# Gram and score products on four quarters of the array, and a mixture layer's activations squared once

## The chip, the cores and the metric

The kernel runs on one core of one Trainium2 chip, as one launch. The metric is the device time of that launch in microseconds (us). Three runs of the kernel before took 984.56, 985.13 and 986.95 us; the median is 985.13 us.

## The reference

Three layers follow one another, on 4 batches of 768 tokens, 8 heads of 48 dimensions (so 384 features):

```python
# delta-rule attention, per head, token by token
k_n = k / (norm(k) + 1e-6)
for t in range(768):
    y[t]  = q[t] @ state
    state = state + beta[t] * outer(k_n[t], v[t] - state.T @ k_n[t])
# first mixture layer, 3072 tokens, 384 -> 2048 -> 384
r = maximum(x @ w_in, 0);  x = (r * r) @ w_out
# second mixture layer: 8 experts, 384 -> 1024 -> 384, one per token
keep = x @ w_skip > 0;  e = argmax(x @ w_gate);  g = max softmax(x @ w_gate)
out = x;  out[keep] += g * (maximum(x @ w1[e], 0) @ w2[e])
```

All data is float32, except that the weights of the first mixture layer come as float64.

## The kernel before

**Attention.** The recurrence is worked in chunks of 64 tokens. A chunk needs, for each head, the 64 by 64 matrix of the keys' products with one another (called G, the Gram matrix) and that of the keys with the queries (P, the scores), both over the 48 dimensions. A *unit* `i` is two chunks, and a *step* `(i, c)` with c from 0 to 3 is one chunk for half of the 32 heads of all batches: 16 heads, held as 8 pairs. There are 6 units, so 24 steps. In a pair one head's 48 dimensions lie on partitions 0 to 47 and the other's on 64 to 111.

`Attn.gram` (lines 241 to 279) makes G and P of one step. `load` (line 249) brings keys and queries of 8 pairs into the tile `gkq`, 128 columns a pair: 64 of keys, then 64 of queries. `spread` (line 253, twice: rows 0 to 47 and rows 64 to 111) copies the keys into the tile `kb`, whose other entries are zero, so that each pair's keys stand block-diagonally as 112 rows by 128 columns. `mm` (line 262), called for each half of the pairs, multiplies: one product of 112 rows gives both heads' G and P as 128 by 128 outputs, four pairs in one PSUM bank. The profile counts two matmul records for a float32 product, so the 8 products of a step are 16 records in two pieces of 8. `copy` (lines 266 and 267) brings G and P into SBUF on ACT, and `store` (line 277) writes the diagonal blocks of G to DRAM.

`sysinv` (lines 297 to 358) takes the blocks of all four steps of a unit back from DRAM (`prep`, line 307), one system to a partition, and inverts them in 31 dependent pairs of DVE instructions (lines 335 and 336). `merge` (products at lines 384 and 398) joins blocks of 32 to blocks of 64. `kv` loads keys and values, and `loadq` (line 426) fetches the queries once more into `qp`, out of the same array as `gkq`: rows of 64 floats with gaps of 64 between them. `recur` holds the four groups of small products of a step, W, U, Y and DS (lines 477, 491, 501, 519). Each of these groups is 16 products and 32 records.

**First mixture layer.** Six units of 512 tokens by 16 slices of the hidden dimension give 96 hidden chunks `f`. `Moe1.w` loads a slice of weights (line 668) and splits it into a rounded part `whi` (ACT, line 672) and a remainder `wlo` (DVE, line 675). `Moe1.h` (lines 698 to 726) makes 9 products into the one PSUM bank `p_h` (line 708), the relu on ACT into the single buffer `r` (713), the rounded square `gh` on ACT (717), the full square `g`, a single buffer, on DVE (721), and the remainder `gl = g - gh` on DVE (724). `Moe1.y` makes 12 products out of `gh`, `gl`, `whi` and `wlo` (738). Weights from float64 are rebuilt as float32 by `Conv.chunk` (lines 548 to 612), 16 chunks on ACT, DVE and POOL, before the first hidden chunk.

**Second mixture layer.** `Moe2` splits the experts' weights and runs sorted blocks of 128 tokens (lines 1051 to 1081).

**What sets the order.** The instructions of attention and first mixture layer are put into one written order per engine by a list scheduler that runs while the kernel is built (`Order`, lines 72 to 166). Each piece has an engine, an estimated duration, an urgency and the pieces it follows; the scheduler steps a model of the engines forward and emits the piece that can start first, the more urgent one among those close together. On the chip each engine's instructions then run in exactly that order. Pieces that write PSUM take banks in rotation: seven (`BANKS`) up to the first hidden chunk, then the three of tag "a". Until then the scheduler also inserts products without use (line 1262) which keep TensorE busy. `schedule` adds attention steps and hidden chunks with urgencies at a fixed spacing `L`, and units 1 to 5 of attention run among the chunks of the mixture layer.

Of the kernel before, what the change touches and what calls it, by code (L numbers as in the profile page):

```python
# [8 lines left out]
F32 = mybir.dt.float32  # L9
# [19 lines left out]
C = 64  # L29
# [42 lines left out]
class Order:  # L72
# [16 lines left out]


    def add(s, urgency, piece, after=(), behind=(), at=0.0):
        k = len(s.p)
        after, behind = tuple(after), tuple(behind)
        s.p.append((urgency, piece, after, behind, at))
        s.n.append(0)
        s.succ.append([])
        for j in (*after, *behind):
            if j not in s.issued:
                s.n[k] += 1
                s.succ[j].append(k)  # L100
        if not s.n[k]:
            s.enable(k)
        return k
# [14 lines left out]
    def run(s, until=None, slack=0.35):  # L118
        todo = set(range(len(s.p)) if until is None else until) - set(s.issued)
        while todo:  # L120
            best = {}
            for k, t in s.ready.items():
                u, (e, d, f, *x), *_ = s.p[k]
                t = max(t, s.free[e])
                if e == PE and x:
                    tag = s.tags[s.turn % len(s.tags)]
                    l = s.taken[tag]
                    if len(l) >= s.count[tag]:
                        j = l[-s.count[tag]] + 1
                        if j not in s.issued:  # L130
                            continue
                        t = max(t, s.end[j])
                best.setdefault(e, []).append((t, u, k))
# [8 lines left out]
            if e == PE:  # L142
                if s.clock:
                    c, n = s.clock, x[1] if len(x) > 1 else 0
                    if t > 54.83 or 3.5 < t < 19.48:
                        b = max(s.free[e], 54.83 if t > 54.83 else 3.5)
                        while c.end(b, 0.11) <= t + 0 or b >= t and c.low(b, d, n):
                            b = c.run(b, 0.11, 256)
                            s.dummy()
                        t = max(t, b)  # L150
                    d = c.run(t, d, n) - t
                if x:
                    s.taken[s.tags[s.turn % len(s.tags)]].append(k + x[0] - 1)
                    s.turn += 1
# [14 lines left out]
class Attn:  # L169


    def __init__(s, ctx, tc, kq, kv, bs, xT, psum):
        s.tc = tc
        s.nc = nc = tc.nc
        s.kq, s.kv_, s.bs, s.xT, s.psum = kq, kv, bs, xT, psum

# [10 lines left out]
        W = 8 * D + 16  # L187
        s.gq, s.gb = ([c1.tile([128, 8, 128], F32, name=f"{n}{i}") for i in range(2)] for n in ("gkq", "kb"))

# [51 lines left out]
    def gram(s, i, ci):  # L241
# [4 lines left out]
        def load():  # L246
            st["q"], st["b"] = s.q0[ci] if i == 0 and ci < 2 else s.gq[ci % 2], s.gb[ci % 2]
            for a in range(2):
                nc.sync.dma_start(out=st["q"][a * 64:a * 64 + D].rearrange("p a b -> p (a b)"), in_=s.kq[c, a, :, h8 * 128:(h8 + 8) * 128])

        def spread(r):
            f = nc.vector.tensor_copy if r and not i else nc.scalar.copy
            f(out=st["b"][r:r + D, :, 64 - r:128 - r], in_=st["q"][r:r + D, :, 0:64])

        def mm(b):
            if b == 0:
                s.P[i, ci] = s.pP.tile([128, 8, 64], F32, name="P")
                s.G[i, ci] = s.pG.tile([128, 8, 64], F32, name="G")
            st[b] = gp = s.psum([128, 4, 128])
            for q in range(4):  # L260
                p = b * 4 + q
# [146 lines left out]
    def kv(s, i, ci):  # L408
# [206 lines left out]
class Moe1:  # L615
# [82 lines left out]
    def h(s, f):  # L698
# [28 lines left out]

# [421 lines left out]

def build(tc, kq, kv, bs, w, wsg, w1, w2, out):  # L1150
    nc = tc.nc
    with ExitStack() as ctx:
# [14 lines left out]
        with ExitStack() as cm:  # L1167
# [19 lines left out]
            cv, tail = cm.enter_context(ExitStack()), cm.enter_context(ExitStack())  # L1187
            A = Attn(ca, tc, kq, kv, bs, xT, psum)
            ew = ctx.enter_context(ExitStack())
# [15 lines left out]
def schedule(A, open_V, open_M, clear, E, free, ca, tail, ew, manual):  # L1205
# [11 lines left out]
    def gram(i, c, ul, u):  # L1217
        m, l = 4 * i + c, A.gram(i, c)
        old = at(gr, m - 2, 5)
        x = [o.add(ul, l[0], old if i else [], at(gr, m - 1, 0))]  # L1220
        x += o.chain(u, l[1:3], x + old)
        x += o.chain(u, l[3:], x[-1:], at(gr, m - 1, 5) + at(mg, m - NG, 2) + at(kv, m - NP, 6))
        gr[m] = x
# [104 lines left out]
    def m_unit(i):  # L1328
        for f in range(NF):
# [72 lines left out]
def layout(q, k, v, beta):  # L1402
# [5 lines left out]

    kq = np.stack([dm(k), dm(q)], axis=4).reshape(12, 2, D, 16 * 128)
    kv = np.stack([tm(k), tm(v)], axis=2)  # L1410
    bs = beta.reshape(2, 2, 4, 2, 6, 2, 2, 32)[:, :, :, ::-1].transpose(4, 6, 5, 0, 3, 1, 2, 7).reshape(6, 128, 32)
    return dict(kq=np.ascontiguousarray(kq), kv=np.ascontiguousarray(kv), bs=np.ascontiguousarray(bs))

# [20 lines left out]
```

## Time and profile before

| | |
|---|---|
| median of three runs | 985.13 us |
| the profiled execution | 984.34 us, span 982.6 us |
| TensorE (PE) busy | 91% |
| VectorE (DVE) busy | 71% |
| ScalarE (ACT) busy | 57% |
| GpSimd (POOL) busy | 34% |
| mean granted TensorE clock | 0.957 |

The span runs from the first to the last instruction; 1.74 us of the profiled execution lie outside it. A busy share is an average over stretches with different limits. Four stretches can be told apart here: attention's first unit and the rebuilding of the weights (0 to 168 us), the mixture layer with the other units of attention (168 to about 645 us), the mixture layer nearly alone (645 to 766 us), and the experts (766 us to the end). PE is matmul, PEld the load of its stationary operand, SP the queue that issues most DMAs.

### The profile page before, as it was taken

What the parts mean: (1) busy time and instruction counts of PE and PEld (TensorE: products, weight loads), DVE (VectorE), ACT (ScalarE), POOL (GpSimd) and SP (SyncE); (2) the same over time, 40 slices, a digit from 0 to 9 for tenths busy, and PEclk for the clock granted to TensorE, in tenths of its full rate; (3) what the DMA queues carried; (4) which work ended last, traced back from release to release, by engine and by line L of the source; (5) the groups of instructions that cost most, each with busy time, mean ns of one, the idle gap of its engine ahead of it and who ended that gap; (6) DMA issues with size and microseconds to landing.
All of it is one profiled execution on the core that took longest, in us unless ns stands there. A gap on an engine that the chain in (4) does not pass through costs nothing. (4 is left out here: it accounts for less than half of the span.)

```text
span 982.6 us, 23182 instructions
## 1 busy us (share of the span) xinstructions
PE 895.4 (91%) x8594; PEld 784.6 (80%) x8594; DVE 695.2 (71%) x1311; ACT 564.3 (57%) x1039; POOL 335.0 (34%) x445
## 2 busy tenths in 40 slices
PE   8577876999989998999989997999999999999996
PEld 6575765887778887888878876888899889898996
DVE  7898677889966998489955998553786523845563
ACT  6824845766577556775576545665665323745562
POOL 9805462134424332433326331531250230111011
PEclk9787996998999999999999999999999999999999
DMA  8937766653586457533765346433591232844661
GB/s 246 271 81 211 226 193 180 159 140 97 141 207 161 113 124 212 153 103 107 195 152 148 94 124 170 108 104 90 171 313 50 72 122 98 292 131 143 226 218 46
DMA packets 148698, 152.12 MB, mean 155 GB/s; under 512 B 92344, under 2 KB 127129, under 8 KB 148560
## 3 DMA queue, kind: packets, MB, share of 16 engines
q1 hardware_dynamic: 132336, 92.84, 33.9%
q0 software_dynamic: 16224, 57.56, 19.9%
q8 instruction: 72, 1.18, 0.5%
q14 instruction: 66, 0.54, 0.2%
HBM read 116.63 MB, written 35.91 MB: 155 GB/s over the span
## 5 line engine op out<-in xcount | busy, mean ns | idle before, releaser
L668 POOL DMA_DIRECT2D wraw<-wc x96 | 53.6, 559 | 293.0 <-DVE wlo L675 203.1
L713 ACT ACTIVATE r<-p_h 128x512 f32<-128x512 f32 x96 | 57.5, 599 | 111.7 <-PE p_h L708 45.6
L672 ACT CAST whi<-wraw 128x778 fp32r<-128x778 f32 x96 | 81.3, 847 | 68.1 <-PE p_y L738 65.2
L675 DVE TENSOR_TENSOR wlo<-wraw,whi 128x778 fp32r<-128x778 f32 x96 | 96.2, 1003 | 24.6 <-ACT whi L672 24.0
L721 DVE TENSOR_TENSOR g<-r 128x512 f32<-128x512 f32 x96 | 66.6, 694 | 56.6 <-ACT r L713 56.4
L738 PE MATMUL p_y<-whi,gl 128*128 128x394 f32 x384 | 88.3, 352 | 6.6 <-DVE gl L724 6.4
L708 PE MATMUL p_h<-xh,wlo 128*128 128x512 f32 x288 | 83.7, 399 | 9.3 <-DVE wlo L675 9.2
L708 PE MATMUL p_h<-xh,whi 128*128 128x512 f32 x288 | 89.2, 418 | 2.5 <-ACT r L713 2.3
L738 PE MATMUL p_y<-whi,gh 128*128 128x394 f32 x384 | 89.5, 355 | 0.0
L738 PE MATMUL p_y<-wlo,gh 128*128 128x394 f32 x384 | 87.2, 350 | 0.0
L336 DVE TENSOR_TENSOR Xsys<-Xsys,Osys 128x31 f32<-128x31 f32 (+15 forms) x186 | 81.8, 440 | 6.4
L335 DVE TENSOR_TENSOR Osys<-Asys,Xsys 128x31 f32<-128x31 f32 (+15 forms) x186 | 80.3, 432 | 3.9
L708 PE MATMUL p_h<-xl,whi 128*128 128x512 f32 x288 | 82.6, 395 | 0.0
L724 DVE TENSOR_TENSOR gl<-g,gh 128x512 fp32r<-128x512 f32 x96 | 71.5, 745 | 15.1 <-ACT gh L717 4.4
L738 PEld LDWEIGHTS p_y<-whi,gl 128*128 128x128 f32 x384 | 71.9, 195 | 9.5 <-DVE gl L724 9.3
L1081 POOL DMA_INDIRECT out<-eo,ex x21 | 23.4, 1116 | 161.8 <-DVEq L979 93.9
L738 PEld LDWEIGHTS p_y<-whi,gh 128*128 128x128 f32 x384 | 69.1, 191 | 6.7
L708 PEld LDWEIGHTS p_h<-xh,wlo 128*128 128x128 f32 x288 | 53.3, 189 | 26.0 <-DVE wlo L675 14.8
L451 POOL TENSOR_TENSOR qp<-P,mask 64x512 f32<-64x512 f32 x48 | 67.9, 1415 | 13.4 <-PE p_a L501 9.5
L738 PEld LDWEIGHTS p_y<-wlo,gh 128*128 128x128 f32 x384 | 72.2, 194 | 0.0
L708 PEld LDWEIGHTS p_h<-xl,whi 128*128 128x128 f32 x288 | 54.5, 189 | 13.0 <-DVE xl L694 0.2
L445 POOL TENSOR_TENSOR x<-x,nw 64x384 f32<-64x384 f32 x48 | 47.0, 980 | 47.3 <-DVE nw L292 44.3
(247 smaller groups left out, 2017.2 us busy)
## 6 DMA issues: line engine op xcount, KB each, us to landing
wraw<-wc POOLq DMA_DIRECT2D x96, 389.0 KB, 3.9
raw<-in_w SPq DMA_DIRECT2D x16, 768.0 KB, 5.2
r<-in_w SPq DMA_DIRECT2D x24, 512.0 KB, 4.8
r<-in_w SPq DMA_DIRECT2D x32, 384.0 KB, 6.1
gkq<-in_kq SPq DMA_DIRECT2D x48, 192.0 KB, 4.1
wc<-cvo SPq DMA_DIRECT2D x16, 389.0 KB, 7.2
ex<-xs SPq DMA_DIRECT2D x24, 193.0 KB, 3.2
k<-in_kv POOLq DMA_DIRECT2D x48, 96.0 KB, 3.8
```

The lines of the kernel that those rows point to most:

```text
L335: v.tensor_tensor(out=tmp, in0=A[:, k, k + 1:32].unsqueeze(2).to_broadcast(sh), in1=X[:, k, None, 0:k + 1].to_broadcast(sh), op=ALU.mult)
L336: v.tensor_tensor(out=X[:, k + 1:32, 0:k + 1], in0=X[:, k + 1:32, 0:k + 1], in1=tmp, op=ALU.subtract)
L445: nc.gpsimd.tensor_tensor(out=x, in0=x, in1=st["n"][r].unsqueeze(2).to_broadcast([64, 8, D]), op=ALU.mult)
L451: nc.gpsimd.tensor_tensor(out=QP[r, 1 - t], in0=P[r], in1=s.mask[r, None, :].to_broadcast([64, 8, 64]), op=ALU.mult)
L668: nc.gpsimd.dma_start(out=st["t"], in_=s.wc[f])
L672: nc.scalar.copy(out=s.W[f][0], in_=st["t"])
L675: nc.vector.tensor_tensor(out=s.W[f][1], in0=st["t"], in1=s.W[f][0].bitcast(F32), op=ALU.subtract)
L708: nc.tensor.matmul(ps, lhsT=w[:, k * 128:k * 128 + 128], rhs=x[k], start=(n == 0), stop=(n == 8))
L713: nc.scalar.activation(out=r, in_=st["p"], func=AF.Relu)
L721: nc.vector.tensor_tensor(out=g, in0=st["r"], in1=st["r"], op=ALU.mult)
L724: nc.vector.tensor_tensor(out=s.g[f][1], in0=st["g"], in1=s.g[f][0].bitcast(F32), op=ALU.subtract)
L738: nc.tensor.matmul(s.ys[t], lhsT=g[:, t * 128:t * 128 + 128], rhs=w[:, DM:], start=first, stop=last)
```

## The change

The Gram products use quarters of the array: each of the 16 heads of a step has its own product, 48 rows by 64 columns of keys against 128 columns of keys and queries. Even pairs go to one PSUM bank and odd pairs to a second; the host exchanges the two heads of every odd pair in the array `kq`, so that the four products of two pairs stand on four different quarters (rows 64 or 0, columns 0 or 64). One piece `mm` takes both banks at once (the new `Order.banks`). The tile `kb`, both `spread` copies and the memsets for them go. The queries for `qp` come from an input of their own, `qf`, without gaps. In the mixture layer ACT makes the full square `g`, and then a second ACT instruction rounds it into `gh`; DVE only makes the remainder.

```diff
@@ class Order
+    def banks(s, n=1):
+        t, used = 0.0, {}
+        for r in range(n):
+            tag = s.tags[(s.turn + r) % len(s.tags)]
+            l, k = s.taken[tag], used.get(tag, 0) - s.count[tag]
+            used[tag] = used.get(tag, 0) + 1
+            if len(l) + k >= 0:
+                if k >= 0 or l[k] + 1 not in s.issued:
+                    return None
+                t = max(t, s.end[l[k] + 1])
+        return t
@@ Attn.init
-        for t in s.q0:
-            nc.vector.memset(t[32:64], 0.0)
-        for t in s.gb:
-            nc.gpsimd.memset(t, 0.0)
-        for i, t in enumerate(s.gq):
-            (nc.vector, nc.gpsimd)[i % 2].memset(t[32:64], 0.0)
@@ Attn.gram
-        def spread(r):
-            f = nc.vector.tensor_copy if r and not i else nc.scalar.copy
-            f(out=st["b"][r:r + D, :, 64 - r:128 - r], in_=st["q"][r:r + D, :, 0:64])
-        def mm(b):
...
-                nc.tensor.matmul(gp[:, q, :], lhsT=st["b"][0:112, p, :], rhs=st["q"][0:112, p, :], start=True, stop=True)
+        def mm():
...
+            st[0], st[1] = s.psum([128, 4, 128]), s.psum([128, 4, 128])
             for q in range(4):
+                for b in range(2):
+                    for a in range(2):
+                        f = (1 - a ^ b) * 64
+                        nc.tensor.matmul(st[b][a * 64:a * 64 + 64, q, :], lhsT=st["q"][f:f + D, 2 * q + b, 0:64], rhs=st["q"][f:f + D, 2 * q + b, :], start=True, stop=True, tile_position=(f, a * 64))
-            nc.scalar.copy(out=G[:, b * 4:b * 4 + 4], in_=gp[:, :, 0:64])
-            nc.scalar.copy(out=P[:, b * 4:b * 4 + 4], in_=gp[:, :, 64:128])
+            nc.scalar.copy(out=G[:, b::2], in_=gp[:, :, 0:64])
+            nc.scalar.copy(out=P[:, b::2], in_=gp[:, :, 64:128])
-        return [(SP, 1.0, load, 1.1), (ACT, 0.45, lambda: spread(0)), (ACT if i else DVE, 0.55, lambda: spread(64)), (PE, 0.87, lambda: mm(0), 1, 1792), (ACT, 0.55, lambda: copy(0)), (PE, 0.87, lambda: mm(1), 1, 1792), (ACT, 0.55, lambda: copy(1)), (SP, 1.9, store, 0.8)]
+        return [(SP, 1.0, load, 1.1), (PE, 0.9, mm, 1, 1536, 2), (ACT, 0.75, lambda: copy(0)), (ACT, 0.75, lambda: copy(1)), (SP, 1.9, store, 0.8)]
@@ Attn.kv
-                nc.sync.dma_start(out=QP[a * 64:a * 64 + D, a], in_=s.kq[c, a, :, h8 * 128:(h8 + 8) * 128].rearrange("p (a w) -> p a w", w=128)[:, :, 64:128])
+                nc.sync.dma_start(out=QP[a * 64:a * 64 + D, a].rearrange("p a w -> p (a w)"), in_=s.qf[c, a, :, h8 * 64:(h8 + 8) * 64])
@@ Moe1.h
-            nc.scalar.activation(out=s.g[f][0], in_=st["r"], func=AF.Square)
+            nc.scalar.copy(out=s.g[f][0], in_=st["g"])
-            nc.vector.tensor_tensor(out=g, in0=st["r"], in1=st["r"], op=ALU.mult)
+            nc.scalar.activation(out=g, in_=st["r"], func=AF.Square)
-        return [(PE, 1.95, mm), (ACT, 0.5, relu), (ACT, 0.55, hi), (DVE, 0.62, sq), (DVE, 0.62, lo)]
+        return [(PE, 1.95, mm), (ACT, 0.5, relu), (ACT, 0.55, sq), (ACT, 0.55, hi), (DVE, 0.62, lo)]
@@ schedule: gram
+        q = o.add(u, l[1], x[:1], at(gr, m - 1, 5) + at(mg, m - NG, 2) + at(kv, m - NP, 6))
+        c0 = o.add(u, l[2], [q])
+        c1 = o.add(u, l[3], [q, c0])
@@ schedule: hidden chunks
-            h.append(o.add(u, l[1], h[:1] + (hs[n - 1][2:4] if n else [])))
-            h.append(o.add(u, l[2], h[1:2] + ([ys[n - 2]] if n > 1 else [])))
-            h.append(o.add(u, l[3], h[1:2] + ([hs[n - 1][4]] if n else [])))
-            h.append(o.add(u, l[4], h[2:4]))
+            h.append(o.add(u, l[1], h[:1] + (hs[n - 1][2:3] if n else [])))
+            h.append(o.add(u, l[2], h[1:2] + (hs[n - 1][3:5] if n else [])))
+            h.append(o.add(u, l[3], h[2:3] + ([ys[n - 2]] if n > 1 else [])))
+            h.append(o.add(u, l[4], h[3:4]))
```

## Rows read from the trace of the kernel before

**Rows 1.** Busy us by stretch: PE, PEld, DVE, ACT, POOL, clock, DMA share, GB/s.
```profile
168.00:645.00 477.00, 447.06 (x5250) 385.69 (x5250) 376.24 (x762) 299.86 (x577) 178.52 (x230) 0.98 0.55 143
645.00:766.00 121.00, 120.65 (x824) 107.79 (x823) 77.33 (x135) 72.10 (x117) 29.70 (x37) 1.00 0.44 139
```
**Rows 2.** Waits, 168 to 645 us: who for whom, us in total, times, longest.
```profile
PE p_h L708 <- DVE wlo L675: 9.2, 11, 1.9
PE p_y L738 <- DVE gl L724: 6.4, 7, 2.2
ACT r L713 <- DVE g L721: 30.8, 11, 4.6
```
**Rows 3.** Timeline of PE, 322 to 325 us: start, us, what; a hidden chunk.
```profile
322.18 0.86 PE L708 MATMUL p_h<-xh,whi 128*128 128x512 f32 x3
...
324.25 0.88 PE L738 MATMUL p_y<-whi,gh 128*128 128x394 f32 x4
```
**Rows 4.** Timeline of PE, 409 to 413 us: the two pieces of a step.
```profile
409.49 1.05 PE L262 MATMUL p_a<-gkq,kb 112*128 112x128 f32 x8
410.47 1.10 PE L477 MATMUL p_a<-lt,k 128*48 128x64 f32 x32
411.50 1.16 PE L262 MATMUL p_a<-gkq,kb 112*128 112x128 f32 x8
412.42 0.94 PE L708 MATMUL p_h<-xh,whi 128*128 128x512 f32 x3
```
**Rows 5.** Timeline of PE, 315 to 318 us: groups on parts of the array.
```profile
315.42 0.69 PE L384 MATMUL p_a<-Tn,G 32*32 32x32 f32 x32
316.04 1.15 PE L501 MATMUL p_a<-qp,x 128*64 128x64 f32 x32
317.13 0.77 PE L398 MATMUL p_a<-lt,Z 32*32 32x32 f32 x32
```
**Rows 6.** Groups of PE by line, 168 to 645 us: count, busy us, mean ns.
```profile
L262 PE MATMUL p_a<-gkq,kb 112*128 112x128 f32 x232 | 32.4, 283 | 0.0
```
**Rows 7.** Timeline of PE, 160 to 168 us: the first hidden chunk.
```profile
161.09 3.62 PE L262 MATMUL p_a<-gkq,kb 112*128 112x128 f32 x16 [5.63 <-ACT kb L253]
164.47 0.94 PE L708 MATMUL p_h<-xh,whi 128*128 128x512 f32 x3
```
**Rows 8.** Timeline of SP, 0 to 40 us.
```profile
2.91 9.53 SPq L249 DMA_DIRECT2D gkq<-in_kq  x8
...
27.70 3.84 SPq L277 DMA_DIRECT2D Ad<-G  x8
...
33.15 0.34 SPq L307 DMA_DIRECT2D Asys<-Ad  x1
```
**Rows 9.** DMA issues, 0 to 40 us: count, KB each, median us to landing.
```profile
gkq<-in_kq SPq DMA_DIRECT2D x12, 192.0 KB, 10.7
```
**Rows 10.** Groups by line, whole span: count, busy us, mean ns, idle before.
```profile
L253 ACT COPY kb<-gkq 48x512 f32<-48x512 f32 x44 | 27.1, 616 | 4.7 <-DMA gkq<-in_kq 4.1
L266 ACT COPY G<-p_a 128x256 f32<-128x256 f32 x40 | 14.8, 370 | 8.8 <-PE p_a L262 8.1
L713 ACT ACTIVATE r<-p_h 128x512 f32<-128x512 f32 x96 | 57.5, 599 | 111.7 <-PE p_h L708 45.6 <-DVE g L721 30.8 <-issue 24.4
L717 ACT ACTIVATE gh<-r 128x512 fp32r<-128x512 f32 x96 | 60.9, 634 | 3.1
L721 DVE TENSOR_TENSOR g<-r 128x512 f32<-128x512 f32 x96 | 66.6, 694 | 56.6 <-ACT r L713 56.4
L724 DVE TENSOR_TENSOR gl<-g,gh 128x512 fp32r<-128x512 f32 x96 | 71.5, 745 | 15.1 <-ACT gh L717 4.4 <-DVE g L721 0.5
L691 ACT CAST xh<-xraw 128x512 fp32r<-128x512 f32 x18 | 10.6, 615 | 2.0 <-DMA xraw<-xT 1.7
L672 ACT CAST whi<-wraw 128x778 fp32r<-128x778 f32 x96 | 81.3, 847 | 68.1 <-PE p_y L738 65.2 <-DMA wraw<-wc 2.4
```
**Rows 11.** DMA issues, whole span: count, KB each, median us to landing.
```profile
qp<-in_kq SPq DMA_DIRECT2D x44, 96.0 KB, 4.1
```

More of the change, by code (lines that the diff above doesn't have):

```diff
@@ L125, in run @@
                 if e == PE and x:
[L126 to L132, printed above, removed]
+                    b = s.banks(*x[2:])
+                    if b is None:
+                        continue
+                    t = max(t, b)
                 best.setdefault(e, []).append((t, u, k))
@@ L151, in run @@
                     d = c.run(t, d, n) - t
-                if x:
-                    s.taken[s.tags[s.turn % len(s.tags)]].append(k + x[0] - 1)
+                for r in range((1, *x[2:])[-1] if x else 0):
+                    s.taken[s.tags[s.turn % len(s.tags)]].append(k + x[0] - 1 + r)
                     s.turn += 1
@@ L169, with __init__ @@
 class Attn:
-    def __init__(s, ctx, tc, kq, kv, bs, xT, psum):
+    def __init__(s, ctx, tc, kq, qf, kv, bs, xT, psum):
         s.tc = tc
         s.nc = nc = tc.nc
-        s.kq, s.kv_, s.bs, s.xT, s.psum = kq, kv, bs, xT, psum
+        s.kq, s.qf, s.kv_, s.bs, s.xT, s.psum = kq, qf, kv, bs, xT, psum
         def pool(n, b, **kw):
@@ L187, in __init__ @@
         W = 8 * D + 16
-        s.gq, s.gb = ([c1.tile([128, 8, 128], F32, name=f"{n}{i}") for i in range(2)] for n in ("gkq", "kb"))
+        s.gq = [c1.tile([128, 8, 128], F32, name=f"gkq{i}") for i in range(2)]
         s.QP = [c1.tile([128, 2, 8, 64], F32, name=f"qp{i}") for i in range(2)]
@@ L246, in load @@
         def load():
-            st["q"], st["b"] = s.q0[ci] if i == 0 and ci < 2 else s.gq[ci % 2], s.gb[ci % 2]
+            st["q"] = s.q0[ci] if i == 0 and ci < 2 else s.gq[ci % 2]
             for a in range(2):
                 nc.sync.dma_start(out=st["q"][a * 64:a * 64 + D].rearrange("p a b -> p (a b)"), in_=s.kq[c, a, :, h8 * 128:(h8 + 8) * 128])
-        def spread(r):
-            f = nc.vector.tensor_copy if r and not i else nc.scalar.copy
-            f(out=st["b"][r:r + D, :, 64 - r:128 - r], in_=st["q"][r:r + D, :, 0:64])
-        def mm(b):
[L256 to L259, printed above, removed]
+        def mm():
+            s.P[i, ci] = s.pP.tile([128, 8, 64], F32, name="P")
+            s.G[i, ci] = s.pG.tile([128, 8, 64], F32, name="G")
+            st[0], st[1] = s.psum([128, 4, 128]), s.psum([128, 4, 128])
             for q in range(4):
-                p = b * 4 + q
-                nc.tensor.matmul(gp[:, q, :], lhsT=st["b"][0:112, p, :], rhs=st["q"][0:112, p, :], start=True, stop=True)
+                for b in range(2):
+                    for a in range(2):
+                        f = (1 - a ^ b) * 64
+                        nc.tensor.matmul(st[b][a * 64:a * 64 + 64, q, :], lhsT=st["q"][f:f + D, 2 * q + b, 0:64], rhs=st["q"][f:f + D, 2 * q + b, :], start=True, stop=True, tile_position=(f, a * 64))
         def copy(b):
             P, G, gp = s.P[i, ci], s.G[i, ci], st[b]
-            nc.scalar.copy(out=G[:, b * 4:b * 4 + 4], in_=gp[:, :, 0:64])
-            nc.scalar.copy(out=P[:, b * 4:b * 4 + 4], in_=gp[:, :, 64:128])
+            nc.scalar.copy(out=G[:, b::2], in_=gp[:, :, 0:64])
+            nc.scalar.copy(out=P[:, b::2], in_=gp[:, :, 64:128])
         def store():
@@ L1147, in run, with build @@
                     s.p2f(b - 1)
-def build(tc, kq, kv, bs, w, wsg, w1, w2, out):
+def build(tc, kq, qf, kv, bs, w, wsg, w1, w2, out):
     nc = tc.nc
@@ L1187, in build @@
             cv, tail = cm.enter_context(ExitStack()), cm.enter_context(ExitStack())
-            A = Attn(ca, tc, kq, kv, bs, xT, psum)
+            A = Attn(ca, tc, kq, qf, kv, bs, xT, psum)
             ew = ctx.enter_context(ExitStack())
@@ L1220, in gram @@
         x = [o.add(ul, l[0], old if i else [], at(gr, m - 1, 0))]
-        x += o.chain(u, l[1:3], x + old)
-        x += o.chain(u, l[3:], x[-1:], at(gr, m - 1, 5) + at(mg, m - NG, 2) + at(kv, m - NP, 6))
+        x += [x[0]] * 2
+        q = o.add(u, l[1], x[:1], at(gr, m - 1, 5) + at(mg, m - NG, 2) + at(kv, m - NP, 6))
+        c0 = o.add(u, l[2], [q])
+        c1 = o.add(u, l[3], [q, c0])
+        x += [q, c0, q, c1] + [o.add(u, z, [c1]) for z in l[4:]]
         gr[m] = x
@@ L1407, in tm @@
         return x.reshape(4, 4, 2, 12, C, D)[:, :, ::-1].transpose(3, 2, 4, 0, 1, 5).reshape(12, 128, 16, D)
-    kq = np.stack([dm(k), dm(q)], axis=4).reshape(12, 2, D, 16 * 128)
+    kq = np.stack([dm(k), dm(q)], axis=4)
+    kq[:, :, :, 1::2] = kq[:, ::-1, :, 1::2].copy()
+    kq = kq.reshape(12, 2, D, 16 * 128)
+    qf = dm(q).reshape(12, 2, D, 16 * C)
     kv = np.stack([tm(k), tm(v)], axis=2)
     bs = beta.reshape(2, 2, 4, 2, 6, 2, 2, 32)[:, :, :, ::-1].transpose(4, 6, 5, 0, 3, 1, 2, 7).reshape(6, 128, 32)
-    return dict(kq=np.ascontiguousarray(kq), kv=np.ascontiguousarray(kv), bs=np.ascontiguousarray(bs))
+    return dict(kq=np.ascontiguousarray(kq), qf=np.ascontiguousarray(qf), kv=np.ascontiguousarray(kv), bs=np.ascontiguousarray(bs))
 def kernel(**inputs):
```

## The prediction

> **What bounds the kernel now.** Read the busy time by stretch first. From 168 to 645 us PE is busy 447.1 of 477 us, from 645 to 766 us 120.65 of 121, while DVE has 376 and 77 us and ACT 300 and 72 [rows 1]. The mixture layer is bound by PE, and only there does a piece taken from PE come back nearly whole, because a hidden chunk is always at hand to move up. The 30 us that PE stands idle from 168 to 645 us are the second thing to read: 9.2 us are waits for `wlo` and 6.4 for `gl`, both made by DVE [rows 2]. The timeline of PE then gives prices from one start to the next: a hidden chunk's 9 products take 2.07 us (322.18 to 324.25) [rows 3], while the two pieces of a Gram step take 0.98 and 0.92 us, 1.90 together [rows 4]. Before 168 us PE is not the bound. There the order is keys, Gram, store, load, inversion on DVE, rebuilt weights, first hidden chunk. After 766 us nothing is changed.
>
> **Gram on quarters, in the layer that PE bounds.** A step goes from 8 products of 112 rows to 16 of 48, from 16 records to 32. No row shows four quarters, so I bound them. A full record with 128 moving columns takes 0.92 / 8 = 115 ns, so one quarter's record takes about that if streaming is all there is. Four quarters at once: 32 x 115 / 4 = 0.92 us. Two at once: 1.84 us. One after the other: 3.68 us. The rows speak against the last: the 32-by-32 group at L384 has two positions of the array, its record streams 32 columns, so 32 x 115 x 32/128 = 0.92 us alone, and it took 0.62 (315.42 to 316.04); the group at L501 streams 64 columns on two column halves, 1.84 us alone, and took 1.09 (316.04 to 317.13) [rows 5]. So two positions overlap almost wholly. The ends are 0.62 us, the fastest group of 32 records, and 3.68. I take the nearest row, 1.09 us: it also loads 64 stationary columns 32 times, and half as many moving columns on half as many positions is the same stream. The step saves 1.90 - 1.09 = 0.81 us. From 168 to 645 us there are 232 records of L262, or 14.5 steps [rows 6]: -11.7 us (ends -18.6 and +25.8).
>
> The rows of L501 show 32 loads of 64 stationary columns and 32 matmuls in 1.09 us, 34 ns for each pair. The Trainium skill, "TensorE: Matmul & The Clock Gate", LDWEIGHTS (loading the stationary operand), has a load take its columns divided by 1.2 in ns, 53 ns for 64 columns, so 32 loads one after the other would be 1.71 us. By that rule the step would save 0.19 us, and the 14.5 steps 2.8 us, not 11.7. The trace of L501 does not agree if loads follow one another, and I go by the trace.
>
> **The step ahead of the first hidden chunk.** A step and its predecessor wait stand directly before the first hidden chunk: PE waits 5.63 us for `kb`, takes 3.38 us for 16 records and starts the chunk at 164.47 [rows 7]. A copy of 0.616 us [rows 10] goes from before it, and 3.38 us shrink as 1.90 to 1.09, by 1.44. If nothing else is late the chunk starts 2.0 us earlier. Something may be (its inputs pass ACT and DVE as well), so 0 to 2.0; I take -1.8, since those inputs are also behind ACT's copies.
>
> **The first unit.** The keys' 8 DMAs are issued from 2.91 to 12.44 us [rows 8] and land 10.7 us after issue at the median [rows 9], so the last come at about 23. The last eight stores run from 27.70 to 31.54, the load of the systems follows at 33.15 [rows 8]. Behind the landing there now lie a copy to `kb`, two pieces of PE and two pairs of ACT copies; then one piece of 1.09 and the same copies. The work removed for the four steps is 4 x 0.81 = 3.2 us on PE and 4 copies each on ACT and DVE. The inversion's start can move up by at most 27.7 - 23 = 4.7 us less one pair of copies of 0.37 [rows 10], at least by nothing if the planned order fills the gap with other work. I take -3, near the PE work removed. Everything up to the first hidden chunk hangs on this inversion, so it is passed on. The memsets that go lie before the keys' landing, hidden by it: 0, and even without that cover their going costs nothing.
>
> **Off the path.** ACT loses 44 copies to `kb`, 27.1 us; it gains an instruction per hidden chunk, priced as a cast of this shape at 0.615 us, 96 x 0.615 = +59 us. DVE loses 66.6 us [rows 10]. In 168 to 645 us ACT comes to about 300 + 43 - 17 = 326 of 460 us, below PE, so the cover is PE's own work. The Gram copies keep their count and size, 0.37 us; if the stride in their output cost as much again, 96 x 0.37 = 36 us on ACT would still be under PE. The queries from `qf` are the same 44 issues of 96 KB, landing in 4.1 us [rows 11]; 0 on PE, since `qp` is needed a whole step later; at best DMA time is freed.
>
> **The chain to `gl`.** Before: relu 0.599, then the slower of 0.634 (ACT) and 0.694 (DVE), then 0.745. After: 0.599 + 0.634 + 0.615 + 0.745. That is 2.59 against 2.04 us, +0.55 [rows 10]. Two products' worth of PE work covers it: 2.07 us of hidden products and a chunk's output products of the same order. Only where PE already waits for `gl`, 7 times [rows 2], is it paid: +3.9 us. Without any cover, 96 x 0.55 = +53. Against it, DVE has 0.694 us less ahead of `wlo`, on which PE waits 11 times for 9.2 us [rows 2]: between 0 and -7.6, I take half, -3.9. The two cancel: 0 (ends -14 and +53). A new wait comes with the single `g`: ACT's square waits for DVE's remainder of the chunk before, and behind it on ACT stand the casts of `whi` and attention's copies, for which PE waits. It replaces ACT's present wait at the relu for DVE's square, 30.8 us in 11 times [rows 2], in the same place, and I price it at nothing beyond that.
>
> **Sum.** -11.7 - 1.8 - 3.0 + 0 = -16.5 us against the profiled execution's 984.34 gives 967.8. The median of the three runs lies 0.8 above that execution, so 968.6 us.
>
> **The rivals.**
> *Quarters overlap only in pairs.* For it: no row shows more than two positions at once. Against it: the new order alternates rows and columns, and each half of a bank is always written from the same rows. The step takes 1.84 us and the gap of a changeover, about the 1.90 of before. Only the first unit's copies and the copy before the first hidden chunk remain: -3.6, so 980.7 us. The Trainium skill, "TensorEngine Tiling (Array Packing)", Gotcha 1: PSUM Pressure, says that different row tiles cannot access one PSUM bank at the same time; here the two products of a pair do write one bank from different rows. That rule would give this case, yet L384 writes one bank from rows 0 and 64 and overlapped (0.62 against 0.92 us), so the trace is against it.
>
> *DVE's relief is worth more.* PE's waits for `wlo` and `gl` go, 15.6 us [rows 2], on top of the sum: 953 us. For it: DVE has 376 of 477 us and its square stands ahead of both. Against it: the longer chain.
>
> *Slower: ACT becomes the late engine for `gl`.* Place: ACT's queue between relu and rounding. Per chunk it has 0.599 + 0.634 + 0.615 + 0.847 (`whi`) = 2.70 us, and from 168 to 645 us attention adds (326 - 69 x 2.70) / 69 = 2.0. Output products follow a chunk's hidden products by about 4.2 us of PE work, the chain takes 2.59, so it decides once 1.6 us of other ACT work stand in between. `whi` and one attention copy are enough for that. If all 69 chunks there then cost 0.55 us, +38 - 16.5: 1006 us. Against it: PE waits for `gl` only 7 times now, and the planned order knows the chain.
>
> *The first unit comes out later.* The list scheduler plans again, with two banks wanted at once; if the gain up to the first hidden chunk turns into a loss of as much (+4.8), the sum is -6.9: 977 us.
>
> **How the numbers follow.** Chances: forecast 0.58 (own range 960 to 976), pairs only 0.15, DVE's relief 0.11, ACT late 0.08, first unit later 0.08. The range 954 to 985 holds the forecast, the pairs, a later first unit and the upper half of DVE's relief, and leaves out ACT late. A change under 0.3% (3.0 us) can't be told from none here: faster is under 982.2, slower over 988.1. Forecast, relief and a later first unit are faster (0.77), and so are 0.06 of the pairs, together 0.83; 0.08 of the pairs are the same; ACT late and the last 0.01 of the pairs are slower, 0.09.
>
> **What would show it.** Right: the Gram piece is one group of 32 records with about 1.1 us to the next start; the stretch with attention shortens by some 12 us with PE as busy as now; the load of the systems comes near 30 us and the first hidden chunk near 160; the relu's wait for DVE is gone. Wrong: a Gram group of 1.8 us or more; PE waits for `gl` that grow beyond 12 us; a first hidden chunk after 164 us.

## The result and the profile after

The changed kernel takes 956.63 us (median of 4 runs, 954.72 to 959.84), the kernel before 986.04 beside it (4 runs): a ratio of 0.970, 95% interval 0.966 to 0.974. Forecast were 968.6, with 954 to 985 as the range. The time lies in that range, but 12 us below the likeliest value and below the 960 to 976 that the forecast gave for itself; the gain is 29.4 us where 16.5 were worked out.

The profiled execution of after took 954.72 us. I call the **layer** the stretch from the first hidden product of the mixture to the first expert product. These rows are the busy times by stretch (columns as in [rows 1]); first the layer in before, then, of after, the two stretches of [rows 1] and the layer.

```profile
164.47:769.42 604.95, 574.66 (x6110) 499.84 (x6110) 457.17 (x900) 375.91 (x701) 208.76 (x267) 0.98 0.53 142
```

```profile
168.00:645.00 477.00, 458.29 (x5814) 393.93 (x5812) 342.98 (x711) 345.39 (x654) 194.12 (x239) 0.99 0.56 148
645.00:766.00 121.00, 117.54 (x634) 102.82 (x631) 61.59 (x150) 73.47 (x125) 33.97 (x40) 1.00 0.43 140
160.99:738.47 577.48, 556.38 (x6353) 480.26 (x6350) 395.49 (x809) 415.12 (x769) 216.52 (x268) 0.99 0.55 149
```

The layer is 27.5 us shorter, the part ahead of it 3.5 (164.47 to 160.99), the part behind it 1.3 longer. In the layer DVE is busy 62 us less and ACT 39 more. PE is idle for 21.1 us of it (577.48 - 556.38) where it was for 30.3. The Gram step, from the timeline of PE (columns as in [rows 3]), answers to [rows 4] and [rows 7]:

```profile
159.08 1.99 PE L264 MATMUL p_a<-gkq 48*64 48x128 f32 x32 [7.80 <-DMA gkq<-in_kq]
160.99 1.65 PE L710 MATMUL p_h<-xh,whi 128*128 128x512 f32 x3
...
164.53 1.10 PE L264 MATMUL p_a<-gkq 48*64 48x128 f32 x32
165.56 0.96 PE L710 MATMUL p_h<-xh,whi 128*128 128x512 f32 x3
```

One group of 32 records now, 1.03 us to the next start (164.53 to 165.56), where the two pieces took 1.90. The first row is the same step at half the clock, 1.91 us: PE had waited 7.80 us ahead of it, no longer for a copy to `kb` but for the keys' DMA. The busy times of the two steps have the granted clock in the third column from the right:

```profile
159.08:160.90 1.82, 1.82 (x32) 1.58 (x32) 1.72 (x5) 0.00 (x0) 0.00 (x0) 0.50 0.20 79
164.53:165.50 0.97, 0.97 (x33) 0.86 (x32) 0.41 (x1) 0.83 (x2) 0.47 (x1) 1.00 0.92 280
```

What PE waits for in the layer (columns as in [rows 2]) has changed places:

```profile
PE p_h L710 <- ACT r L715: 8.4, 6, 2.4
PE p_h L710 <- DVE wlo L677: 3.7, 4, 2.8
...
PE p_y L740 <- ACT gh L719: 1.5, 2, 1.3
...
PE p_a L386 <- DMA Tn<-Tnd: 0.2, 1, 0.2
```

In before the layer had 9.2 us for `wlo`, 6.4 for `gl` [rows 2], and for a DMA (`Tn`) and ACT's relu:

```profile
PE p_a L384 <- DMA Tn<-Tnd: 5.3, 4, 1.8
PE p_h L708 <- ACT r L713: 2.3, 3, 1.0
```

Now `wlo` has 3.7, `gl` 0.1, `Tn` 0.2, and the relu leads with 8.4. Of the groups by line in the layer (last columns: count, busy us, mean ns, then the idle time ahead of the group on its engine and what ended it), these answer to [rows 6] and [rows 10]:

```profile
L740 PE MATMUL p_y<-whi,gl 128*128 128x394 f32 x384 | 85.5, 344 | 0.1
...
L726 DVE TENSOR_TENSOR gl<-g,gh 128x512 fp32r<-128x512 f32 x96 | 78.7, 820 | 108.1 <-ACT gh L719 107.9
...
L723 ACT ACTIVATE g<-r 128x512 f32<-128x512 f32 x96 | 60.6, 632 | 7.1 <-DVE gl L726 4.2 <-DVE Osys L337 0.2
L719 ACT CAST gh<-g 128x512 fp32r<-128x512 f32 x96 | 59.6, 621 | 3.0
L715 ACT ACTIVATE r<-p_h 128x512 f32<-128x512 f32 x96 | 57.2, 596 | 86.0 <-PE p_h L710 85.5
...
L264 PE MATMUL p_a<-gkq 48*64 48x128 f32 x484 | 18.3, 277 | 0.0
```

The relu's wait for DVE's square, 30.8 us in 11 times [rows 2], is gone. The new wait that the prediction named, ACT's square for DVE's remainder of the chunk before, is 4.2 us. DVE now stands 107.9 us idle ahead of the remainder: it has room.

From one start to the next, the layer's 27.5 us are: Gram 10.0 (26.9 to 16.9 us), idle PE 9.2 (30.3 to 21.1), half clock 5.6, and 2.7 that remain for the other products. The half clock is counted from the granted clock in sixty equal stretches of the layer: 20.6 us at 1.2 GHz before, 9.4 after, and each such microsecond is put down as costing half of itself (the Gram step above took 1.91 us there and 1.03 at the full clock). About 0.7 us stand in two of these terms: one Gram piece of before took 1.70 us (228.89 to 230.59), most of it at half the clock, where the others took 0.81 to 0.98.

### The profile page after: what moved, and what is told of

Its sections match the earlier page's. It is cut to its first block, busy times and chain, and to the rows that moved or that the text cites. A ratio compares the mean times of both kernels' runs of the same rounds, so it can differ in the third digit from the quotient of the medians.

```text
span 953.0 us, 23830 instructions
## 1 busy us (share of the span) xinstructions
PE 871.9 (91%) x8974; PEld 754.4 (79%) x8974; DVE 630.5 (66%) x1208; ACT 592.3 (62%) x1091; POOL 337.9 (35%) x442
## 5 line engine op out<-in xcount | busy, mean ns | idle before, releaser
L726 DVE TENSOR_TENSOR gl<-g,gh 128x512 fp32r<-128x512 f32 x96 | 78.7, 820 | 108.1 <-ACT gh L719 107.9
L677 DVE TENSOR_TENSOR wlo<-wraw,whi 128x778 fp32r<-128x778 f32 x96 | 102.1, 1063 | 16.8 <-ACT whi L674 16.2
L740 PE MATMUL p_y<-whi,gl 128*128 128x394 f32 x384 | 85.5, 344 | 0.1
L740 PE MATMUL p_y<-wlo,gh 128*128 128x394 f32 x384 | 84.7, 342 | 0.0
L453 POOL TENSOR_TENSOR qp<-P,mask 64x512 f32<-64x512 f32 x48 | 78.6, 1638 | 16.2 <-PE p_a L503 13.1
L338 DVE TENSOR_TENSOR Xsys<-Xsys,Osys 128x31 f32<-128x31 f32 (+15 forms) x186 | 78.1, 420 | 6.4
L337 DVE TENSOR_TENSOR Osys<-Asys,Xsys 128x31 f32<-128x31 f32 (+15 forms) x186 | 74.3, 400 | 3.9
L740 PEld LDWEIGHTS p_y<-wlo,gh 128*128 128x128 f32 x384 | 70.1, 189 | 0.0
L723 ACT ACTIVATE g<-r 128x512 f32<-128x512 f32 x96 | 60.6, 632 | 7.1 <-DVE gl L726 4.2
L710 PEld LDWEIGHTS p_h<-xh,whi 128*128 128x128 f32 x288 | 49.4, 189 | 19.4 <-ACT r L715 10.5
```

The source lines that it names most:

```text
L337: v.tensor_tensor(out=tmp, in0=A[:, k, k + 1:32].unsqueeze(2).to_broadcast(sh), in1=X[:, k, None, 0:k + 1].to_broadcast(sh), op=ALU.mult)
L338: v.tensor_tensor(out=X[:, k + 1:32, 0:k + 1], in0=X[:, k + 1:32, 0:k + 1], in1=tmp, op=ALU.subtract)
L453: nc.gpsimd.tensor_tensor(out=QP[r, 1 - t], in0=P[r], in1=s.mask[r, None, :].to_broadcast([64, 8, 64]), op=ALU.mult)
L677: nc.vector.tensor_tensor(out=s.W[f][1], in0=st["t"], in1=s.W[f][0].bitcast(F32), op=ALU.subtract)
L710: nc.tensor.matmul(ps, lhsT=w[:, k * 128:k * 128 + 128], rhs=x[k], start=(n == 0), stop=(n == 8))
L723: nc.scalar.activation(out=g, in_=st["r"], func=AF.Square)
```

## The experiments

All are compared with before by runs on the same chip; rows of the table come in part from different chips, on which before itself took 983.3 to 986.0 us. Their profiled executions are compared in one table, since the argument needs the same four numbers of each (us in the layer; "half" is the time at 1.2 GHz).

```
kernel            median  ratio (95%)            layer  PE idle  half  DVE busy  ACT busy
before            986.0   1                      605.0   30.3    20.6    457       376
queries_only      985.7   0.999 (0.996, 1.002)   606.5   32.6    18.8    458       375
replan            987.6   1.003 (1.000, 1.006)   610.3   34.3    27.5    462       375
gram_only         972.9   0.990 (0.987, 0.993)   598.7   30.6    32.5    460       358
gram_two_r        973.2   0.989 (0.985, 0.994)   603.0   36.0    29.7    458       358
after_dve_load    971.9   0.987 (0.982, 0.993)   596.3   32.5    32.6    456       417
squares_only      962.6   0.978 (0.976, 0.981)   580.7   17.3     7.0    394       432
after             956.6   0.970 (0.966, 0.974)   577.5   21.1     9.4    395       415
after_again       956.6   0.972 (0.967, 0.977)   578.6   21.9    10.8    395       416
quarters_pairs    959.0   0.975 (0.972, 0.978)   589.9   22.8    21.2    394       415
quarters_serial   976.9   0.990 (0.982, 0.997)   592.4   15.9    11.1    392       418
after_costs       953.0   0.969 (0.963, 0.974)   578.7   21.1    17.9    393       417
```

### The parts by themselves

**gram_only** is the changed kernel with the squares as they were: ACT rounds the square of `r`, DVE squares it once more.

```diff
-            nc.scalar.copy(out=s.g[f][0], in_=st["g"])
+            nc.scalar.activation(out=s.g[f][0], in_=st["r"], func=AF.Square)
...
-            nc.scalar.activation(out=g, in_=st["r"], func=AF.Square)
+            nc.vector.tensor_tensor(out=g, in0=st["r"], in1=st["r"], op=ALU.mult)
```

> The change's Gram part alone (quarters, no copies to kb, the queries' own input); the squares stay as before, rounded square on ACT, full square on DVE. Theory A (parts add): PE work falls by some 16 us between the first hidden chunk and the experts, and the first hidden chunk comes 3.5 us earlier, but PE's waits for DVE's remainders (9.2 for wlo, 6.4 for gl) stay: 966 to 970 us. Rival B (the waits went because the whole order was planned anew): those waits fall here too, below 8 us together, and the time is under 962. Rival C (the gain is the squares'): over 975.

Measured: 972.9 us, 13.1 less than before. The waits in its layer, of PE:

```profile
PE p_h L710 <- DVE wlo L677: 8.2, 6, 1.9
PE p_a L264 <- DVE x L526: 4.6, 1, 4.6
PE p_a L386 <- DMA Tn<-Tnd: 4.4, 4, 1.8
PE p_y L740 <- DVE gl L726: 3.3, 6, 1.0
```

DVE's waits stay, and PE is as idle as before (30.6 us). Gram's 9 us (26.9 to 18.0) come back only in part in the layer (6.2), while the half clock grew from 20.6 to 32.5 us. Over whole runs, too, the mean granted clock was lower, 0.943 in the six runs of gram_only against 0.954 in the 17 of before beside them. So the array's quarters by themselves give less (13.1 us) than the forecast gave them (16.5), not more.

**squares_only** is the kernel before with only the squares moved: the same two lines the other way, in before.

```diff
-            nc.scalar.activation(out=s.g[f][0], in_=st["r"], func=AF.Square)
+            nc.scalar.copy(out=s.g[f][0], in_=st["g"])
...
-            nc.vector.tensor_tensor(out=g, in0=st["r"], in1=st["r"], op=ALU.mult)
+            nc.scalar.activation(out=g, in_=st["r"], func=AF.Square)
```

> The change's square part alone on the kernel before: ACT makes the full square and rounds it, DVE only the remainder; Gram as before. Theory A: DVE's relief takes away most of PE's 15.6 us of waits for wlo and gl, and some time at the lower clock, and adds a few us of waits for ACT: 970 to 975 us, with the first hidden chunk where it was (164 us). Rival B (waits went by the new order): PE's idle time between the first hidden chunk and the experts stays near 30 us and the time is 981 to 990. Rival C (ACT becomes late once its copies to kb are still there): slower than before.

Measured: 962.6 us, 23.4 less than before, more than was expected. Its layer by busy time and by PE's waits:

```profile
165.40:746.10 580.70, 563.43 (x6110) 494.30 (x6110) 393.56 (x804) 431.83 (x797) 218.38 (x267) 0.99 0.55 148
```

```profile
PE p_h L708 <- ACT r L713: 7.5, 6, 1.7
...
PE p_y L738 <- DVE gl L724: 1.5, 1, 1.5
...
PE p_h L708 <- DVE wlo L675: 0.6, 2, 0.3
```

The layer has lost 24.2 us without one PE instruction fewer (6110 as before): idle time -13.0, half clock -13.6, which is 6.8 of time; the other 4.4 are spread over the products. Its six whole runs had a mean granted clock of 0.959, before's 0.954. The larger part of the whole gain sits here, in the edit that was priced at nothing.

**replan** changes none of the work: the list scheduler, which orders the pieces, gets another slack, and so another order.

```diff
-    def run(s, until=None, slack=0.35):
+    def run(s, until=None, slack=0.40):
```

> The kernel before with the same instructions, but written in another order: the scheduler's margin between pieces that start close together is 0.40 in place of 0.35 us. Theory A (the waits of PE are a matter of DVE's load): within 4 us of 985, PE idle 25 to 35 us between the first hidden chunk and the experts. Rival B (any new order moves this kernel by as much as the unexplained 12 us): over 6 us away on either side.

Measured: 987.6 us, 0.3% over before. Its idle time is 34.3 us. One other order with the work of before brought nothing, which speaks against a lucky order as the cause of squares_only's gain, though one order can't exclude it.

**queries_only** is before with the queries from their own input.

```diff
-... in_=s.kq[c, a, :, h8 * 128:(h8 + 8) * 128].rearrange("p (a w) -> p a w", w=128)[:, :, 64:128])
+... in_=s.qf[c, a, :, h8 * 64:(h8 + 8) * 64])
```

> The kernel before, with the queries' tile loaded from an input of their own (one row of 512 contiguous numbers per partition) in place of every second 64 numbers of the joint input; Gram and squares as before. Theory of the forecast (the load is needed a whole step later, PE does not wait for it): 0, a ratio of 1.000 within 0.003. Rival (the smaller packets take the DMA engines from transfers that PE waits for, such as the 5.3 us of waits for Tn): the number of packets falls by about 17000, PE's waits for DMAs fall from 5.3 us to under 1 and the time by about 5 us, a ratio of 0.995.

Measured: 985.7 us, no change. The DMA lines of its page, against 148698 packets before, and PE's waits:

```profile
DMA packets 133914, 152.12 MB, mean 154 GB/s; under 512 B 75448, under 2 KB 110233, under 8 KB 133776
```

```profile
PE p_h L708 <- DVE wlo L675: 9.4, 11, 1.9
PE p_y L738 <- DVE gl L724: 6.5, 8, 2.2
PE p_a L384 <- DMA Tn<-Tnd: 5.9, 3, 2.2
```

14784 packets are gone, all that the change takes, and the waits stand as they were, the one for `Tn` too. That `Tn` no longer delays PE in after is therefore not the queries' doing.

### What the squares do: DVE's load or the coupling

Two things go with the squares. DVE has 0.694 us less per chunk, so `wlo`, `gl` and attention's pieces come earlier; or it is that `r` is free sooner, since nobody on DVE reads it any more, and ACT's relu no longer waits for DVE.

**after_dve_load** is the changed kernel with a product of 128x512 on DVE for each chunk, whose result nobody reads. It has DVE's load back but not the coupling through `r`.

```diff
+        def extra():
+            t = s.c1.tile([128, 512], F32, name="xx")
+            x = s.xh[0].bitcast(F32)
+            nc.vector.tensor_tensor(out=t, in0=x, in1=x, op=ALU.mult)
...
+            o.add(u, l[5], h[1:2])
```

> The changed kernel with an instruction without use on DVE for each hidden chunk, a product of 128x512 of the input's rounded part with itself, as long as the square that left DVE (0.69 us), and planned like it. It neither reads the relu's buffer nor is read by anyone. Theory E (DVE's load is what PE waited for): PE's waits for wlo come back to 8 us or more, PE idle between first hidden chunk and experts to about 30, time 966 to 972 us. Rival F (the coupling: the relu's single buffer was held by DVE's square, 30.8 us of waits on ACT): the time stays within 4 us of 957.

Measured: 971.9 us, 15.3 more than after beside it (956.6), and about what gram_only takes. Its layer:

```profile
164.00:760.30 596.30, 563.80 (x6352) 487.32 (x6349) 455.69 (x905) 416.96 (x769) 220.19 (x268) 0.97 0.53 144
```

```profile
PE p_h L710 <- ACT r L715: 11.0, 4, 5.5
PE p_a L264 <- DVE x L526: 5.5, 1, 5.5
PE p_h L710 <- DVE wlo L677: 3.7, 4, 1.7
```

DVE is back at 455.7 us, PE's idle time at 32.5 and the half clock at 32.6. The load as such takes the gain away. It does not return at the place it left: the wait for `wlo` is 3.7 us as in after. It comes as a longer wait for the relu and one for attention's `x`. That DVE's pieces come a little later everywhere is the reading of this; they were not followed one by one.

**gram_two_r** is gram_only with a second buffer for `r`, so that the relu need not wait for DVE's square.

```diff
-            st["r"] = r = s.c1.tile([128, 512], F32, name="r")
+            st["r"] = r = s.p2.tile([128, 512], F32, name="r")
...
-            h.append(o.add(u, l[1], h[:1] + (hs[n - 1][2:4] if n else [])))
+            h.append(o.add(u, l[1], h[:1] + (hs[n - 2][2:4] if n > 1 else [])))
```

> The kernel with the Gram part alone, and the relu's buffer doubled, in the plan too, so that the next relu need not wait for DVE's square; the square stays on DVE. Theory E (DVE's load): no gain over the Gram part alone, 970 to 976 us. Rival F (coupling): the relu's waits for DVE go, PE's idle time falls from 31 towards 20 us, and the time to 958 to 964.

Measured: 973.2 us, the same as gram_only. Of ACT's waits in its layer the two for the relu and the cast of the weights lead, and no wait for DVE's `g` is left (it had 32.1 us in gram_only):

```profile
ACT r L715 <- PE p_h L710: 113.5, 85, 3.4
ACT whi L674 <- PE p_y L740: 73.6, 73, 2.3
```

```profile
PE p_h L710 <- DVE wlo L677: 9.3, 8, 1.9
```

The coupling was taken away, and PE is idle for 36.0 us. The theory of the coupling falls. The prediction was right that ACT's 30.8 us at the relu cost PE nothing.

### What a Gram step is made of

**quarters_pairs** is the changed kernel with the products of a step in the sequence b, q, a: eight products on two diagonal quarters, which write one bank from different rows, then eight on the other two.

```diff
-            for q in range(4):
-                for b in range(2):
+            for b in range(2):
+                for q in range(4):
                     for a in range(2):
```

> The changed kernel with the 16 Gram products of a step in another sequence: first the 8 of one bank, which alternate between two quarters, then the 8 of the other bank. Theory A (streams on four quarters run at once, and only neighbours in the sequence overlap): a step's group takes 1.8 to 1.9 us to the next start in place of 1.0; 15 steps in the mixture layer and a little in the first unit make 969 to 973 us. Rival D (a group is bound by its 32 loads of 64 columns, about 34 ns each): the group stays at 1.0 to 1.1 us and the time at 956.

**quarters_serial** goes on to b, a, q: four products of one quarter, then four of the next.

```diff
-            for b in range(2):
-                for q in range(4):
-                    for a in range(2):
+            for b in range(2):
+                for a in range(2):
+                    for q in range(4):
```

> The changed kernel, with the 16 products of a Gram step issued quarter by quarter: the four products of one quarter of the array in a row, then the four of the next. The sequence b, q, a, with two quarters active at a time, took 1.52 us from start to next start, and the changed kernel's sequence over all four takes 1.03. Theory I (a quarter's own stream is what takes the time, and only products of different quarters that stand next to each other overlap): a record of 128 moving columns takes 115 ns alone, 32 of them 3.7 us, a step near 3.5 us; the layer's 16 steps cost 16 x 2.5 = 40 us more than in the changed kernel, 995 us and a ratio near 1.01. Theory J (the 48 rows or the 64 columns of a quarter make a record short, whatever stands next to it): about 1.5 us a step as with two quarters, 960 us. The step's time to the next start decides, the total only bears it out.

One step of each on PE's timeline, the pairs first:

```profile
267.26 1.59 PE L264 MATMUL p_a<-gkq 48*64 48x128 f32 x32
268.78 0.99 PE L740 MATMUL p_y<-whi,gh 128*128 128x394 f32 x4
```

```profile
280.51 2.56 PE L264 MATMUL p_a<-gkq 48*64 48x128 f32 x32
283.01 0.98 PE L740 MATMUL p_y<-whi,gh 128*128 128x394 f32 x4
```

To the next start: 1.03 us with all four quarters in turn, 1.52 with two, 2.50 with one. Neither sequence took what was expected of it (1.8 to 1.9 or 1.0 to 1.1 for the pairs, 3.5 or 1.5 for the serial one). Single records show why. In the first unit the two banks of a step have different names, `p_a` and `p_y`, so the timeline keeps their records apart. First the serial sequence, where the last quarter of `p_a` meets the first of `p_y`, then after, where two quarters write each bank; both at the full clock:

```profile
15.69 0.32 PE L264 MATMUL p_y<-gkq 48*64 48x128 f32 x1
15.80 0.27 PE L264 MATMUL p_a<-gkq 48*64 48x128 f32 x1
15.85 0.27 PE L264 MATMUL p_y<-gkq 48*64 48x128 f32 x1
15.90 0.27 PE L264 MATMUL p_a<-gkq 48*64 48x128 f32 x1
15.96 0.27 PE L264 MATMUL p_y<-gkq 48*64 48x128 f32 x1
```

```profile
14.85 0.28 PE L264 MATMUL p_a<-gkq 48*64 48x128 f32 x2
14.86 0.28 PE L264 MATMUL p_y<-gkq 48*64 48x128 f32 x2
14.96 0.28 PE L264 MATMUL p_a<-gkq 48*64 48x128 f32 x2
14.97 0.28 PE L264 MATMUL p_y<-gkq 48*64 48x128 f32 x2
```

The records of one quarter start about 0.11 us apart, with another quarter beside it (15.80, 15.90; 15.85, 15.96) and with three (14.85, 14.96). A quarter with none beside it is no faster: the serial step starts four records in its first half microsecond (busy time of PE and PEld with their records, clock, DMA share, GB/s):

```profile
280.50:281.00 0.50, 0.49 (x4) 0.49 (x5) 1.00 1.03 288
```

So a record on a quarter is about as long as a full one (0.92 / 8 = 0.115 us), and what the step gains (1.90 to 1.03) is that four quarters run abreast: it lasts little longer than the eight records of one quarter. The serial step is not 32 x 0.11 = 3.5 us, because a quarter starts before the one ahead of it is through: at 15.69 records of `p_a` are still to come. Theory I was right in what takes the time and wrong in that only neighbours overlap. Rival D falls: the same 32 loads took 1.52 and 2.50 us in other sequences.

The Trainium skill, "TensorEngine Tiling (Array Packing)", Gotcha 1: PSUM Pressure, says that different row tiles cannot access one PSUM bank at the same time; here the trace disagrees: in the rows of after above, the two `p_a` records of a line come from different rows and go into one bank, and such a pair starts every 0.11 us, as a single record of one quarter does.

The times follow the step loosely: the pairs take 959.0 us, 2.4 over after and not clear of the noise, the serial sequence 976.9, 20.2 over. In the serial sequence's profiled execution (981.17 us) Gram takes 20.6 us more of the layer than in after (16.9 to 37.5), and the layer is only 14.9 longer, because PE waits 5.2 us less. Another 11.8 us lie ahead of the layer, which starts at 172.82: the longer steps of the first unit come before the load of the systems, which now stands 9.7 us later than in after (30.09, shown below).

```profile
39.80 0.50 SPq L309 DMA_DIRECT2D Asys<-Ad  x1
```

### A version beyond after

**after_costs** is the changed kernel with the planner's costs set to measured durations, for the hidden chunk, the casts of the weights and the output products. **after_again** is after itself, run beside it.

```diff
-        return [(PE, 1.95, mm), (ACT, 0.5, relu), (ACT, 0.55, sq), (ACT, 0.55, hi), (DVE, 0.62, lo)]
+        return [(PE, 2.07, mm), (ACT, 0.6, relu), (ACT, 0.63, sq), (ACT, 0.62, hi), (DVE, 0.75, lo)]
...
-        return (PE, 2.0, mm)
+        return (PE, 2.17, mm)
```

> The changed kernel planned with the durations that the trace shows for a hidden chunk: 2.07 and 2.17 us on PE, relu 0.60, square 0.63, rounding 0.62, remainder 0.75, whi 0.85, wlo 1.03 (they stood at 1.95, 2.0, 0.5, 0.55, 0.55, 0.62, 0.75, 0.9). Theory E: the plan then places relu and remainder where they really are, PE's waits for the relu (8.4 us) and wlo (3.7) halve, 948 to 954 us. Rival B (any new order may win or lose some us): 952 to 964 with other waits in their place.

> The changed kernel once more, as it is, beside the others on the same chip: 955 to 959 us. If time at the half clock differs from execution to execution, the profiled execution's share of it need not be the 9 us of the first profile, and a longer execution has more of it.

Measured: 953.0 us against 956.6, with ratios to before whose intervals overlap (0.963 to 0.974 and 0.967 to 0.977). The relu's wait did not halve:

```profile
PE p_h L710 <- ACT r L715: 9.5, 6, 2.6
```

The layer is as long as in after_again (578.7 and 578.6); what differs is its start, 159.0 against 163.0 us. It is the lowest of all medians, but 3.6 us from after are not settled by six runs each, and the reason that it was made for failed.

## Why the prediction was right, and where not

**The Gram step: right.** 1.09 us was taken from the nearest row, 1.03 is measured ahead of a hidden chunk, and the mechanism, quarters that run abreast, held. 11.7 us were forecast for the stretch with attention, and 10.0 came out in the whole layer, 9.3 without the piece at half the clock. The price of a step was a little high: 1.90 [rows 4] was one of the dearer steps. The 15 steps in the layer took 1.79 us on the mean before (26.9 / 15) and 1.13 after (16.9 / 15), since a step ahead of other small products can take longer (1.46, from 289.43 to 290.89); each saved 0.67 us where 0.81 was worked out. The 115 ns of a record on its quarter were close to the measured 0.11 us. The ends were too far: one after the other is 2.50 us, not 3.68, and pairs take 1.52, not 1.84, because a quarter starts before the one ahead of it is through. The rival of the pairs falls on the chip, since all four quarters overlap; a step as long as with pairs would have cost about 2.4 us against after, not the 12 between 980.7 and the forecast.

**The way to the first hidden chunk: right, a little high.** -4.8 was forecast for it, -3.5 measured. The load of the systems is where it was looked for, near 30 us; SP's timeline (answering to [rows 8]):

```profile
16.77 9.81 SPq L279 DMA_DIRECT2D Ad<-G  x16
...
30.09 0.50 SPq L309 DMA_DIRECT2D Asys<-Ad  x1
```

That is 3.06 us earlier than 33.15 [rows 8], the -3.0 of the first unit. The step ahead of the chunk shrank as forecast, from 3.38 to 1.91 us, both times at half the clock (granted clock 0.51 and 0.50). But it starts only 2.0 us earlier (161.09 to 159.08), because PE now waits 7.80 us ahead of it for the keys: the 3.0 of the first unit and the copy did not arrive there whole. The first hidden chunk itself moves between executions, 160.99 and 163.0 in two of after, 164.47 in before and 168.4 in queries_only, which does the same up to there but for the queries' loads; so a microsecond or two of this term can't be told.

**Off the path: right for the queries, not quite for ACT.** The queries are worth nothing, as forecast. 39 us more on ACT in the layer, priced at nothing, go with 6.1 us more of PE's waits for the relu; they are counted in the next step. The rival that made ACT late for `gl` said that `whi` and one attention copy fill 1.6 us of ACT; by [rows 10] they make 0.847 + 0.370 or 0.847 + 0.616, 1.2 to 1.5 us, so it needed two copies.

**The chain to `gl` and DVE's relief: the step that failed.** The prediction set +3.9 for a longer chain against -3.9 for DVE's relief: "The two cancel: 0 (ends -14 and +53)". The chain did not get dearer: PE's waits for `gl` went from 6.4 to 0.1 us. The waits for `wlo` fell by 5.5 and those for `Tn` by 5.1, which was in no term. Back came 6.1 at the relu and 1.5 at `gh`. Together PE is idle for 9.2 us less. On top of it 11.2 us less of the layer run at half the clock, 5.6 us, and a term for the clock was nowhere in the sum. In the sum of the steps, then: Gram -10.0, start -3.5, this step -14.8 (idle PE and half clock), other products -2.7, the part behind the layer +1.3, in all -29.7, against 954.72 - 984.34 = -29.6.

The rival with ACT late for `gl` falls with that wait, and the one with a later first unit with the load at 30.09. The mechanism is that of the rival "DVE's relief is worth more" (953 us, 0.11), and the time lies in the wide range because that range took in a part of this rival. That its 953 came within 4 us is in part luck: of its 15.6 us of waits 11.8 went, 5.1 of `Tn` went too, 7.6 came back under ACT's name, and 5.6 of half clock were in no sum. That DVE's load is what counts, squares_only and after_dve_load show from both sides: take the square from DVE alone and 23.4 us go, put the load back alone and 15.3 return.

The error was to price DVE's relief too narrowly. Each wait for `wlo` was let fall by one square at most (0.694 us), and half of that was taken; with the square gone from DVE alone the waits went from 9.2 to 0.6 us. And DVE at 457 of 605 us also delayed a wait under another name: that for `Tn`, which goes with the square (0.3 us in squares_only) and stays without it (4.4 in gram_only, 5.9 in queries_only).

**What stays open.** The parts don't add up: 13.1 and 23.4 us alone, 29.4 together. After the squares have moved, Gram's quarters take 10.7 us from PE in the layer (27.6 to 16.9), but the layer shortens by 3.2 only, with 3.8 us more of idle PE and 2.4 more at half the clock. That ACT is then the late engine is the reading (the relu leads PE's waits in squares_only and in after), not shown: no run relieved ACT. Nor is it settled how much of the half clock belongs to each kernel. In the layer it is 19 to 33 us in the six profiled executions with DVE at 456 us or more, and 7 to 21 in the six with less, so the ranges touch. Over whole runs the mean granted clock was 0.953 in before (11 runs) and 0.952 in after (6 runs beside them), so the 5.6 us hold for the layer of these executions only. In other kernels the whole runs do differ: 0.942 in after_dve_load and 0.943 in gram_only, 0.959 in squares_only (6 runs each).

## What to carry to other kernels

An engine at three quarters of the time of a stretch that another engine bounds is not free: price its relief by trying it, for the waits that carry its name hold only a part of what its lateness costs. Small products on quarters of the array pay in full only if the sequence keeps all four quarters busy; the same sixteen products took 1.03, 1.52 or 2.50 us by their sequence alone. And gains measured one by one need not add: 13.1 and 23.4 us made 29.4.

## What the runs showed of the hardware that was not expected

Records of 48 rows, 64 stationary and 128 moving columns start about 0.11 us apart on their quarter, in float32 and at the full clock, whether none, one or three other quarters run beside it. In the serial sequence the next quarter's first record starts (15.69) while the former still has records to come (15.80, 15.90).

The spread of one kernel goes mostly with the half clock. The 13 runs of before beside quarters_serial go from 980.37 us at a mean granted clock of 0.959 to 993.53 at 0.942: 980.37 x 0.041 = 40.2 and 993.53 x 0.058 = 57.6 us would be lost to it, 17.4 apart, and the times are 13.2 apart.

The same instruction on DVE, the remainder of 128x512, has a median of 692 ns in after and of 693 in before, but a mean of 820 and of 745 [rows 10], and single ones up to 1791. With less load on DVE its instructions did not become shorter on the mean; what delays the long ones was not tried.
